# Linear attention with adaptive layer norm and an MLP: kv from sums of normalised rows, and a planned k and q stage

## The chip, the core and the metric

The kernel runs on one core of a Trainium2 chip. Five engines work side by side, each through its own instructions in order: TensorE (PE; its weight loads are PEld), VectorE (DVE), ScalarE (ACT), GpSimd (POOL) and SyncE (SP), which here issues nearly all transfers. The metric is the device time of one execution in microseconds (us), as the median of several runs.

## The reference

The input x has 2048 rows of D = 576. A vector c gives six rows of modulation by `silu(c) @ w_mod`. There are 32 heads of 18 columns; phi(t) is t + 1 above zero and exp(t) below, plus 1e-6.

```python
mod = silu(c) @ w_mod                       # sa, ca, ga, sb, cb, gb
h = layernorm(x) * (1 + ca) + sa
q, k, v = split(h @ wqkv)                   # 32 heads of 18
kv = einsum("bhsd,bhse->bhde", phi(k), v)   # per head 18 x 18
z = einsum("bhsd->bhd", phi(k))
o = einsum(phi(q), kv) / (einsum(phi(q), z) + 1e-6)
x = x + ga * (o @ wo)
h = layernorm(x) * (1 + cb) + sb
x = x + gb * (silu(h @ w1) @ w2)            # w1 is 576 x 4608
```

Everything is fp32 at the interface. The large products are made from operands that are split into a rounded high part and a remainder ("hi" and "lo"), and three products of the parts.

## The kernel before

Rows are worked in 16 tiles of 128 (`NT`), and four tiles make a block of 512 (`NB` = 4). The 576 columns are four chunks of 128 and one of 64 (`KC` = 4). A projection of a tile is 14 passes over pairs of such parts, each on two halves of the output columns: 28 matmuls (`x_passes`, L298).

The program has four stretches.

1. **Start** (`start_of_work` on, L538). The first rows of modulation are summed for the columns `cols["a"]`, tiles 0 to 3 are normalised, and k of tiles 0 and 1 is projected while weights arrive. `load_w` (L391) loads all of `wqkv` here: k, v and q, 1.33 MB each.
2. **k, v, q** (the loop at L870). For each tile t: `k_proj` (L698), phi(k) and its split into `pk` (`k_split`, L452); `v_proj` (L703), and v's split into `vx`, six small operations on ScalarE and VectorE out of PSUM; then `kv_mm` (L723) for the tile before, ten matmuls of 256 columns that gather v^T phi(k) over all 16 tiles in three PSUM tiles, `kvp`; and one `q_proj` (L718), whose phi goes to `acc[t]`. In between, the next block's rows are loaded (`load_block`), normalised, turned by 32x32 transposes and a way through DRAM (`turn_block`, L353: four stores, eight fetches), modulated and split into `hT` (`turn`, L747). The other rows of modulation are made by the way: `mod_piece` (L654) sums five scaled pieces of `w_mod` on VectorE and stores them to DRAM, `mod_sum` (L670) gathers them back in runs of nine elements and adds them up, giving `vec`. `find_first` (L838) reads all of two groups' MLP weights to find the scale factors.
3. **End of attention** (L926 to L1006): the last `kv_mm`, the mask and the row z from the PSUM sums, `kvm`, and M = kvm x (wo x ga) in five steps (L991 to L1000), with q of tiles 8 to 10 in between.
4. From L1011 on, the output of attention, its second layer norm and the MLP. The MLP's second part is emitted by a list scheduler, `Schedule` (L1832): each operation is added with an engine, a time that the planner counts for it, names that it reads and writes, and a lag for transfers. `emit` runs a model of the five engines and issues, on each, the ready operation with the earliest due time; TensorE keeps the order given.

In stretches 1 to 3 the order on TensorE is the order of the program text (`manual_schedule`). The orders on the other engines are lists of numbers written out by hand, `FIRST` (L99) for stretches 1 and 2 and `ORDERS` (L67) for what follows. An engine works strictly in that order: an instruction that waits holds those behind it.

Of the kernel before, what the change touches and what calls it, by code (L numbers as in the profile page):

```python
# [24 lines left out]
def kernel(ctx: ExitStack, tc, A_x, A_wqkv, A_wo, B_x, B_w1, B_w2, c, w_mod, out):  # L25
# [33 lines left out]
    def behind(instructions):  # L59

        with ExitStack() as order:
# [7 lines left out]
            0 2-3 5 4 1 6-12 16-18 14 13 15 19-21 23-25 32-33 26 34 22 27 44-46 28-30 40 53 35 54-55 31 36 63 47  # L69
            64-65 37-39 72 48-51 73 41 56 74 52 82 57-58 66 59-61 83-84 94 62 67 95 42 68-70 75 96 106 71 76 43 107  # L70
            77 86 80 108 81 85 88 87 78 92 79 89-91 115-116 97 93 117 126 98-102 127 103-105 109 128 145 110 146
            111-112 114 113 118 147 164-165 119-121 123-124 122 132 131 129 134 125 139 133 138 130 142 150-151 141
            161 166 162 135-136 152-153 137 163 167 154-155 173-175 156 168 158 160 172 143-144 148-149 176 157 159
            177 140 182 169-171 178-179 185 181 180 183-184 187-191 186 195 192 194 196 193 197-201 205 204 203 202
            206-207 210 209 208 211 225 229 212 221-223 233 230 234 236 235 227-228 237 214-215 238-240 216 213
            217-220 245 224 241 244 231-232 249 246 226 248 247 250 252 251 257 261 242-243 254-255 258 256 253
            259-260 262-263 265 264 268 266-267 269 273 270-272 278 274-277 281 280 282-285 279
        """,
        "Activation": """
            0-5 7 6 8-10 12 11 13-18 20 19 25-26 21 24 22-23 28-29 32 30-31 41 34 36 38 40 33 35 42 45 43 37 39 44 27  # L80
            46 48 50 52 47 53 49 51 54-57 60 58-59 69-70 62 64 66 71-73 68 61 63 65 67 74-77 81 83 82 84 79 78 85-87
            89 95 80 90 88 100-104 91-92 97 99 93-94 105 96 98 106-108 110 112-113 109 111 114 119-120 116 118 115
            117 121 123 122 124-125 127 129-131 128 126 132-134 144 146 136-138 135 139-143 145 147 150-153 156
            148-149 157-160 166 171 161-164 167 154-155 169-170 168 165 174 173 175 172 176-179 181 180 182-183 185
            187-189 186 190-192 184 194 193
        """,
        "Pool": """
            4 0-3 5-10 17 11 14 12-13 18 15-16 21 19-20 25 22-23 28 31 26-27 34 29 24 30 38 32-33 41 35-36 44 39-40
            68 56 37 42-43 60 45-46 63 47-48 51 57 52 58 49 53 50 55 54 61-62 59 64-66 78 67 69 73-75 70 76 71 77 72
            84 83 86 88 85 87 91-92 82 79 89-90 94 93 97 95-96 98-99 101 80 103 100 104 102 106 81 105 107-111  # L90
        """,
        "SP": """
            0-1 4-6 2-3 8-9 7 10-12 15 13-14 16-18 25 22 20 19 21 27-28 24 26 23 29-32 34 33 36-37 35 40 49 39 41-42
            38 43-47 50-51 53 52 48
# [6 lines left out]
            0 2 1 4-5 3 6-21 24-25 22-23 26 28 27 29-30 43-44 31-32 46 33-34 47 35-37 40 38 45 48-49 39 41-42 51 50  # L101
            53 52 55 54 56-58 61 60 62 88 63 89-90 64-65 68-69 71-72 70 73-75 77-78 76 79-80 91 66-67 81-87 93 59 92
            94-96 152 97 99-101 103-104 106-107 98 110-112 102 105 109 113-114 108 127-128 130-131 129 132-133 116
            134 136-137 135 138-139 115 117 140-141 119 142 120 143 121 144-146 118 122-123 153-154 124-125 155 126
            147-151 156-159 161 160 162-164 193-194 196-197 195 198-200 165 202-203 201 204-205 167 171 206-207 168
            208-212 172-174 166 175 169-170 176-184 190-191 185 192 213-215 186 219 216-217 223 187 218 220 224 221
            234 222 238 188-189 231-233 235-237 240-248 225 249-253 230 254-257 239 227 226 258-259 228 260 229
            261-263
        """,
        "Activation": """  # L110
            0-4 6-7 5 8-10 13 11-12 14-18 21 19-20 22-25 27 29 31 30 32 26 28 34 33 41-43 37 39 36 48 38 40 50 52 44
            46 56 45 57 47 49 58 51 53 35 59 54-55 60-62 65-67 70 73 63 68 64 77 71 78 69 79 75 72 80 76 81 74 82-83
            85 91 86 92 87 84 88-90 93-99 104 101 100 102 107 103 105 111 108 112 116 106 117 109 126-127 113-115 110
            118-125 128-130 133 138 134 140 131 139 144 132 141 149 135 145 136 150 137 142-143 146-148 151-170
        """,
        "Pool": """
            0-1 3-4 2 6-7 5 8-12 15-17 13-14 18-20
        """,
        "SP": """
            0-31 33 32 62 34-38 40-41 39 42-45 48-49 47 46 63-65 50-53 66 54 56-57 55 70-73 58-61 67-68 78-79 84-88  # L120
            90-91 89 92-95 80-82 69 74-77 83 96 99 98 100-102 97 106 103-105
# [87 lines left out]
    warm = pa.tile([P, 1], F32, name="warm")  # L209
    crowp = pa.tile([P, P], F32, name="crow")  # L210
    crow = crowp[: KC + 1]
    fixed = const.tile([P, 8], F32, name="fixed")
    BOUNDS, ALPHA, SINV, GINV = fixed[:, 0:2], fixed[:, 2:3], fixed[:, 3:4], fixed[:, 4:5]
# [18 lines left out]
    wkvs = [t[:, i * 2 * D : (i + 1) * 2 * D] for t, n in ((w7, 3), (w5, 2), *((t, 2) for t in wg2)) for i in range(n)]  # L232
    wq = wqp.tile([P, 2 * KC + 1, D], F32R, name="wq")


    class LayerNorm:


        def __init__(self, pool):
            self.mv = pool.tile([P, 4, 2], F32, name="mv")  # L240
            self.ve = pool.tile([P, 4], F32, name="ve")
            self.rstd = pool.tile([P, 4], F32, name="rstd")
            self.nm = pool.tile([P, 4], F32, name="nm")
            self.pool = pool
# [70 lines left out]
    def wkv(b):  # L315

        return wkvs[b]

    def wqp_(b):
        return wq[:, b, :]  # L320
# [4 lines left out]
    kvp = [psA.tile([P, 2, 256], F32, name=f"kvp{i}") for i in range(3)]  # L325

    def psT():
        t = psA.tile([P, 512], F32, name="psT")
        return t
# [5 lines left out]
    def rows4():  # L335
        t = pa.tile([P, 4, DX], F32, name="xt")
        return t

    def load_x(i):
        xt = x0[:, i]  # L340
        nc.sync.dma_start(xt[:, :D], x[i * P : (i + 1) * P, :])
        return xt

    def load_block(tb):
        xx = rows4()
        for a in range(4):
            src = x[tb * 512 + a * P : tb * 512 + (a + 1) * P, :].rearrange("(t j) d -> j t d", t=4)
            nc.sync.dma_start(xx[32 * a : 32 * a + 32, :, :D], src)  # L350
        return xx

    def turn_block(tb, xx):  # L353

        sq = accb[NB - 1].rearrange("p a d -> p (a d)").rearrange("p (f q) -> p f q", q=P)
        for t in range(4):
            V.transpose(sq[:, :, 32 * t : 32 * t + 32], xx[:, t, :D].rearrange("p (f i) -> p f i", i=32))
        room = dram.tile([32, D // 32, 4, P], F32, name=f"turned{tb}")
        for a in range(4):
            nc.sync.dma_start(room[:, :, a, :], sq[32 * a : 32 * a + 32])  # L360
# [45 lines left out]
    for j in (1, 2):  # L406
        load_w(j, START)
# [1738 lines left out]
```

## Time and profile before

| | |
|---|---|
| median of 3 runs | 1129.71 us (1128.67 to 1131.22) |
| the profiled execution | 1127.2 us |
| its span, first to last instruction | 1125.5 us |
| TensorE's granted clock, mean | 0.994 |
| busy: PE, DVE, ACT, POOL | 1083.3, 899.7, 692.8, 662.5 us |
| stretches 1 to 3 end (first transpose of the attention output) | 238.1 us |

The page of the profile lists the busy time of each engine, the granted TensorE clock, the chain of work that ended last, and the costliest groups of instructions as "line engine op out<-in xcount | busy, mean ns | idle before, and what ended it". The table by stretches gives busy time by engine for any part of the span. A wait is put down to the one thing that came last. Lines are those of the kernel before.

### The profile page before, as it was taken

The page shows a single profiled execution, that of the slowest core. Times are in us where ns is not written, and L with a number is a line of the kernel's source. Part 1 is how long each engine was busy: PE and PEld are TensorE (multiplying, and loading weights), DVE is VectorE, ACT ScalarE, POOL GpSimd, SP SyncE. Part 2 cuts the span into 40 slices and gives each one's busy share as a digit, 9 for nine tenths or more (in the row PEclk, how much of TensorE's full clock was granted, in tenths as well). Part 3 has the DMA queues.
Part 4 walks back from the last instruction along what each step waited for, and adds up shares of the span by engine and source line. Part 5 has one row for each costly group of instructions (what it writes and reads, how often), then busy time and mean ns, then how long its engine had stood idle before and what let it go on. Part 6 is the DMA issues. An engine that isn't in the chain of part 4 may idle for free.

```text
span 1125.5 us, 19357 instructions
## 1 busy us (share of the span) xinstructions
PE 1083.3 (96%) x7137; PEld 778.4 (69%) x7137; DVE 899.7 (80%) x1478; ACT 692.8 (62%) x1336; POOL 662.5 (59%) x759
## 2 busy tenths in 40 slices
PE   8999799999999997999999999999999999999998
PEld 6899798899888554566666666666666666666665
DVE  7757574678698889989898888897897897898857
ACT  4643452244755668777677677686686686676654
POOL 3300000065462468968979858878778778777563
PEclk9999899999999999999999999999999999999999
DMA  9376958223344565858757757747757657725522
GB/s 293 81 198 156 129 139 105 43 67 112 122 102 139 200 232 174 281 129 262 205 183 224 219 166 242 223 147 240 215 156 241 219 149 240 222 82 176 172 86 106
DMA packets 120079, 193.53 MB, mean 172 GB/s; under 512 B 43372, under 2 KB 78064, under 8 KB 119984
## 3 DMA queue, kind: packets, MB, share of 16 engines
q1 hardware_dynamic: 119812, 191.99, 58.9%
q8 instruction: 56, 0.92, 0.4%
q14 instruction: 39, 0.32, 0.1%
q10 hardware_dynamic: 172, 0.30, 0.1%
HBM read 176.77 MB, written 15.48 MB: 171 GB/s over the span
## 4 chain that ended last, share of the span: by engine, by line
PE 75%; DMA 8%; DVE 6%; POOL 4%; ACT 4%; issue 1%; SPq 1%; POOLq 0%; ACTq 0%; DVEq 0%
PE up L1595 29%; PE down L1679 28%; PE big L302 7%; PE psK L302 4%; DMA z<-in_B_w_dram 2%; DMA acc<-in_A_wqkv_dram 2%; PE small L1103 1%; DMA xt<-in_A_x_dram 1%; PE big L1114 1%; DMA turned<-acc 1%; PE psK L997 1%; PE big L1028 1%; PE small L287 1%; DVE st L249 1%; PE kvp L729 1%
## 5 line engine op out<-in xcount | busy, mean ns | idle before, releaser
L1595 PE MATMUL up<-hT,w 128*128 128x512 f16 x1264 | 316.7, 380 | 8.3 <-DMA hT<-hd 3.3
L1595 PEld LDWEIGHTS <-w 128*128 128x128 f16 x1492 | 146.1, 98 | 142.5 <-issue 9.7
L1688 DVE SCALAR_TENSOR_TENSOR acc<-acc,set,down 128x576 f32<-128x576 f32 x128 | 103.5, 810 | 33.8 <-PE down L1679 32.9
L302 PE MATMUL psK<-w,hT 128*128 128x256 f32 (+1 forms) x638 | 106.8, 305 | 14.2 <-DVE vx L177 13.1
L1613 ACT ACTIVATE f<-f,set 128x512 f32<-128x512 f32 x102 | 73.3, 719 | 61.5 <-DVE f L1619 51.5
L1633 POOL TENSOR_TENSOR s<-f,f 128x256 f32<-128x256 f32 x66 | 54.8, 830 | 92.0 <-ACT f L1614 89.7
L302 PEld LDWEIGHTS psK<-w,hT 128*128 128x128 f32 x638 | 95.4, 197 | 15.4 <-issue 14.0
L1679 PE MATMUL down<-w,hb 128*128 128x288 f16 x600 | 88.9, 286 | 2.5 <-DVE U L1690 1.7
L1679 PE MATMUL down<-w,hc 128*128 128x288 f16 x600 | 88.9, 286 | 0.2 <-DVE acc L1692 0.2
L1679 PE MATMUL down<-w,hT 128*128 128x288 f16 x480 | 82.8, 286 | 0.4 <-DVE acc L1692 0.4
L1617 DVE TENSOR_TENSOR f<-up,p 128x512 f32<-128x512 f32 x102 | 69.6, 682 | 13.7 <-PE up L1595 8.3
L1679 PEld LDWEIGHTS <-hb 128*128 128x128 f16 x600 | 58.7, 98 | 24.6 <-issue 2.8
L1614 ACT ACTIVATE f<-f,set 128x512 f32<-128x512 f32 x102 | 73.6, 722 | 3.3
L1679 PEld LDWEIGHTS <-hc 128*128 128x128 f16 x600 | 58.7, 98 | 21.9 <-issue 0.5
L255 POOL TENSOR_TENSOR rstd<-ve,neghalf 128x4 f32<-128x4 f32 (+3 forms) x10 | 9.9, 993 | 103.4 <-DVE ve L254 102.3
L1657 POOL TENSOR_TENSOR hc<-s,hc 128x512 f16<-128x512 f32 x50 | 63.1, 1262 | 5.6 <-ACT hc L1653 5.6
L1619 DVE TENSOR_TENSOR f<-up,f 128x512 f32<-128x512 f32 x68 | 46.8, 688 | 24.5 <-PE up L1595 23.8
L1679 PEld LDWEIGHTS <-hT 128*128 128x128 f16 x480 | 47.0, 98 | 26.6 <-issue 0.8
L1637 POOL TENSOR_TENSOR f<-f,s 128x256 f32<-128x256 f32 x66 | 53.0, 803 | 17.1 <-DVE hb L1657 9.4
L1630 POOL TENSOR_TENSOR s<-f 128x256 f32<-128x256 f32 x66 | 56.3, 853 | 7.2 <-ACT f L1610 4.8
L1635 POOL TENSOR_TENSOR s<-s,f 128x256 f32<-128x256 f32 x66 | 56.6, 857 | 3.5
L1679 PE MATMUL down<-w,hd 128*128 128x288 f16 x396 | 55.1, 288 | 0.0
(381 smaller groups left out, 2698.2 us busy)
## 6 DMA issues: line engine op xcount, KB each, us to landing
hT<-hd SPq DMA_DIRECT2D x101, 640.0 KB, 4.7
hT<-hd SPq DMA_DIRECT2D x65, 512.0 KB, 4.0
hT<-in_B_w_dram SPq DMA_DIRECT2D x14, 576.0 KB, 6.7
hT<-in_B_w_dram SPq DMA_DIRECT2D x28, 256.0 KB, 6.3
raw<-in_B_w_dram SPq DMA_DIRECT2D x9, 576.0 KB, 6.8
v<-in_B_w_dram SPq DMA_DIRECT2D x9, 576.0 KB, 4.9
xt<-in_A_x_dram SPq DMA_DIRECT2D x16, 288.0 KB, 5.5
raw<-in_w_mod_dram SPq DMA_DIRECT2D x8, 576.0 KB, 7.8
```

The lines of the kernel that those rows point to most:

```text
L302: T.matmul(ps, xpart(a), wpart(b), start=n == 0, stop=n == len(XW) - 1)
L1595: T.matmul(ps, left, right, start=first and m == 0, stop=m == len(seq) - 1, skip_group_check=True)
L1613: A.activation(f, f, AF.Silu, scale=factor(self.g, "inv"))
L1614: aside(A.activation(f, f, AF.Identity, scale=factor(self.g, "delta")))
L1617: V.tensor_add(f, self.bank[bank[1]], self.p1)
L1630: G.tensor_sub(self.s3, half(i, 0, 0), half(i, 0, 1))
L1633: G.tensor_add(self.s[:, 0:1], half(i, 0, 1), half(i, 1, 1))
L1635: G.tensor_sub(self.s[:, 1:2], self.s[:, 0:1], half(i, 0, 0))
L1637: G.tensor_sub(half(i, 1, 0), half(i, 1, 0), self.s[:, 1:2])
L1657: eng.tensor_sub(t[:, :, 1, :], src, t[:, :, 0, :])
L1679: T.matmul(ps[:, p, :HALF], left[:, u, p * P : (p + 1) * P], right[:, v], start=n in (1, 5, 7, 6) and j == 0, stop=j == len(passes) - 1, s ...
L1688: V.scalar_tensor_tensor(dst, dst, factor(self.g, "ratio"), ps[:, :, :HALF], op0=ALU.mult, op1=ALU.add)
```

## The change

Since v = h Wv, and h is a normalised row times (1 + ca) plus sa, the sum of v^T phi(k) over rows can be made without v. The changed kernel sums, over all rows, the products of normalised rows (before modulation) and phi(k): a 576 x 576 matrix in five tiles `sums_of`, in SBUF. It applies (1 + ca), the term of sa times z, and Wv once, at the end. In detail:

- `v_proj`, `vx` and `kv_mm` go. `split_rows` splits the normalised rows of a block into hi and lo (`xs`), one ScalarE copy and two subtractions per tile, the wide one on VectorE for two tiles and on POOL for two.
- After the k tiles of a block, `sum_steps` makes five chunks of 24 (or 16) matmuls of 288 columns over its four tiles, in two PSUM tiles `psG` by turns, and adds each to `sums_of`.
- `zsum` collects phi(k) by POOL adds; `z_steps` sums it over partitions by a matmul with ones, and corrects `sums_of` by z times sa.
- `kv_steps` multiplies with Wv in fp32: 25 matmuls of 126 columns. Wv is loaded late (`load_late`), so only the weights of k and q are loaded at the start.
- `mod_steps` scales the pieces of `w_mod` on ScalarE and adds them on POOL, where `mod_piece` did both on VectorE.
- Stretches 2 and 3 are emitted by `Schedule`, which moves up in the text unchanged. TensorE's order is: q0, q1, k2, k3, q2, sums of block 0, q3, k4 to k7, q4, sums of block 1, k8 to k11, q5 to q7, sums of block 2, k12 to k15, q8, sums 0 and 1 of block 3, z, sums 2 to 4, q9, kv, q10, M.
- A tile of x or PSUM is used again under names: x of the next block may load when `split_rows` and the transposes have read the last; `xs` is written again when the sums have read it; k and q tiles use two PSUM tiles, K0 and K1, by turns.
- Blocks 1 to 3 keep their rows in another order (`rows_of`), also where x is loaded again and the result is stored; the MLP's `store` is two transfers in place of one.
- The lists `FIRST` and `ORDERS` are shorter by what the planner has taken over.

In the order that this gives, the gather of the first modulation piece stands on SyncE after the store of turned block 2 and ahead of its eight fetches, and its reduction (into `crow`) on VectorE between the two modulates and the five splits of block 2. The gather of the second piece stands behind block 3's fetches, six scan loads and the store of the parts; its reduction stands on VectorE between the first phi operation (PSUM to `a`) of k12 and its second, ahead of those of k13.

The diff, cut to its core:

```diff
-    for j in (1, 2):
-        load_w(j, START)
+    load_w(1, START)
...
+    def project(t, wpart):
+        ps, k = k_bank()
...
+            pe(0.264 * n, product, [x for x in names if x.split(".")[1][0] == str(c)], [k])
+    def phi_steps(ps, k, out, names):
+        do("ACT", 0.65, lambda: A.activation(halves(e_), ps[:, :, :HALF], AF.Exp), [k], ["e"])
+        do("DVE", 0.75, lambda: V.tensor_scalar(halves(out), ps[:, :, :HALF], 0.0, EPS, op0=ALU.max, op1=ALU.add), [k], names)
+        do("DVE", 0.79, lambda: phi_out(e_, out), ["e"], names)
+    def k_steps(t):
...
+        do("ACT", 0.68, lambda: A.copy(pk[i][:, 0], a), [an], [f"pkh{i}"])
+        by_pool = i < 2 or t == 2
+        eng, us = (G, 1.6) if by_pool else (V, 0.75)
...
+        do("POOL", 1.6, lambda: G.tensor_add(zsum, zsum, a), [an], ["zsum"])
+    def split_rows():
+        C = KC * P
+        for t in range(4):
+            do("ACT", 0.68, lambda t=t: A.copy(xs[t][:, :D], xt[:, t, :D]), [f"xt{t}"], [f"xhi{t}"])
+            eng, us = (V, 0.7) if t < 2 else (G, 1.35)
...
+    def block_steps(b):
+        for t in range(4):
+            do("SP", 0.1, lambda t=t: nc.sync.dma_start(xt[:, t, :D], rows_of(x, 4 * b + t)), [], [f"xt{t}"], 6.5)
...
+        do("SP", 0.4, store, SQ, [f"turned{b}"], 4.7)
+        do("SP", 0.4, fetch_main, [f"turned{b}"], XT, 4.5)
+        do("SP", 0.4, fetch_tail, [f"turned{b}"], [XTAIL], 5.5)
+    def sum_steps(b, c):
+        ps, g = g_bank()
...
+                    T.matmul(ps[:, h, :HALF], l, pk[t][:, u, h * HALF : (h + 1) * HALF],
+                             start=t == 0 and m == 0, stop=t == 3 and m == len(left) - 1)
...
+    def mod_steps(piece):
...
+                do("ACT", 1.25, lambda raw=raw, kp=kp, scale=scale: A.activation(raw[:kp], raw[:kp], AF.Identity, scale=scale), [], raws2[i])
+                do("POOL", 2.7, lambda raw=raw, dst=dst, kp=kp: G.tensor_add(dst, dst, raw[:kp]), raws2[i], ["tmod"])
+        do("SP", 0.1, lambda: nc.sync.dma_start(parts, tmod2[:, :, 0:D]), ["tmod"], [f"parts{piece}"], 5.5)
+        i = next(of_raw) % 2
+        r = raw2[i].rearrange("q a d -> q (a d)").rearrange("q (p j) -> q p j", j=NC9)
+        do("SP", 0.1, lambda: nc.sync.dma_start(r, parts.rearrange("p a d -> p (a d)").rearrange("p (q j) -> q p j", j=NC9)),
+           [f"parts{piece}"], raws2[i], 8.0)
+        s9 = s9s[piece - 1]
+        do("DVE", 2.27, lambda: V.tensor_reduce(s9, r.rearrange("q p j -> q j p"), axis=AX.X, op=ALU.add), raws2[i], [f"s9{piece}"])
...
+    def kv_steps():
+        ps, g = g_bank()
+        def product(j):
+            n = HG if j < NHC - 1 else TAIL
+            o = ps[:n, 0, j * HG : (j + 1) * HG] if j < NHC - 1 else ps[:n, 1, :n]
+            for c in START:
+                T.matmul(o, wvs[c][:, j * HG : j * HG + n], sums_of[c][:, j * HG : j * HG + n], start=c == 0, stop=c == KC)
...
         def store(self, b, i, k):
-            t0 = (4 * b + 2 * i) * P
-            dst = of[t0 : t0 + 2 * P, k * HALF : (k + 1) * HALF]
-            nc.sync.dma_start(dst.rearrange("(i p) d -> p i d", p=P), self.c(b, i, k))
+            for u in range(2):
+                nc.sync.dma_start(rows_of(of, 4 * b + 2 * i + u, slice(k * HALF, (k + 1) * HALF)), self.c(b, i, k)[:, u])
```

848 lines of the change are left out of this document (460 added, 388 removed).

## The prediction

> **What bounds the kernel now.** I read the page first, then the chain that ended last, then the table by stretches of the first 238 us (the part that changes), TensorE's waits there, and SyncE's queue in order of time. Page and stretches (columns: us, then busy us and instruction count of PE, PEld, DVE, ACT, POOL, then clock, DMA share, GB/s):
>
> ```profile
> span 1125.5 us, 19357 instructions
> PE 1083.3 (96%) x7137; PEld 778.4 (69%) x7137; DVE 899.7 (80%) x1478; ACT 692.8 (62%) x1336; POOL 662.5 (59%) x759
> 75.00:100.00 25.00, 22.09 (x166) 21.68 (x166) 20.73 (x39) 8.81 (x19) 1.37 (x1) 1.00 0.47 145
> 100.00:120.00 20.00, 15.28 (x118) 15.08 (x116) 8.28 (x14) 7.18 (x16) 0.00 (x0) 1.00 0.88 177
> 120.00:136.80 16.80, 14.11 (x95) 13.90 (x95) 11.80 (x29) 7.24 (x15) 1.29 (x1) 0.90 1.02 110
> 136.80:186.00 49.20, 49.20 (x361) 49.07 (x362) 31.72 (x48) 20.06 (x42) 2.34 (x5) 0.97 0.79 128
> 186.00:220.30 34.30, 29.64 (x209) 28.82 (x208) 18.59 (x43) 8.58 (x22) 0.60 (x1) 0.95 0.33 78
> sum 204.70, PE 187.81 PEld 182.91 DVE 128.98 ACT 81.20 POOL 22.59; mean PE 23.48 PEld 22.86 DVE 16.12 ACT 10.15 POOL 2.82
> 120.00:125.00 5.00, 5.00 (x26) 5.00 (x27) 4.84 (x16) 3.60 (x7) 0.00 (x0) 0.66 1.77 60
> PE psK L302 <- DVE vx L177: 13.1, 4, 4.7
> 136.80 9.20 PE psK L302 x56
> 146.00 1.19 PE kvp L729 x10
> 147.18 7.49 PE psK L302 x56
> 225.37 2.21 PE psK L997 x8
> 231.31 6.80 PE psK L997 x28
> 238.11 0.55 PE big L1028 x5
> ```
>
> TensorE bounds it. The sum row (33.4 to 238.1 us) has it busy for 187.81 of 204.70 us; its 16.9 idle us lie in a few holes, 13.1 of them behind VectorE's v rows. A hole is paid twice: after the 4.7 us one the granted clock is 0.66 for 5 us (1.7 us lost), and the first 56 matmuls after another take 9.20 us where 7.49 is usual. From 238.11 on, the attention output and the MLP follow; the change leaves their work alone, so I move 238.11 and keep the rest.
>
> **The change, part by part.**
>
> TensorE's work. A projection of one 128-row tile is 28 matmuls, half of the 7.49 row: 3.74 us. The 16 v projections go; the 16 tiles' sums cost 28 matmuls of 288 columns each: the same, so nothing. The 16 kv groups of 10 go: 16 x 1.19 = 19.0 us. Added: 25 fp32 matmuls of 126 columns for kv. The chain's L997 rows show fp32 as two instructions per matmul, at 2.21/8 = 0.276 us with 288 columns; five 128-column transposes take 0.55, 0.11 each. So 50 instructions cost 5.5 to 13.8 us; I take 6.0, as 0.276 x 126/288 = 0.12 lies by the lower row. The z row stays two such matmuls. Net -13 us.
>
> In the new order TensorE has 14 k and 11 q projections (93 us), 16 sum tiles (60), M (2.21 + 6.80 = 9.0), kv 6.0, z 1.1, ten transposes 1.1: 170 us. It starts with transposes of tiles 2 and 3, which wait for this row:
>
> ```profile
> 28.11 2.29 ACT L264 ACTIVATE xt<-xt,nm,rstd 128x64 f32<-128x64 f32 x4
> 29.29 0.28 PE L302 MATMUL psT<-w,hT 128*128 128x256 f32 x1
> ```
>
> so at 30.4 (before, the first v tile, the PE row, began at 29.3), and without holes M would end near 200.5. The rest is holes: TensorE takes its instructions in the listed order, and so do the others, so a wait at the head of VectorE's or SyncE's queue holds whatever stands behind it. These rows price the chains that make them (groups by form, the table of DMA issues, the chain, SyncE's queue):
>
> ```profile
> L177 DVE TENSOR_TENSOR hT<-acc,hT 128x512 fp32r<-128x512 f32 x12 | 8.2, 688 | 3.9 <-ACT hT L278 3.8
> L437 DVE TENSOR_SCALAR a<-psK 128x576 f32<-128x576 f32 x15 | 11.3, 755 | 15.2 <-ACT e L432 15.0
> L665 DVE SCALAR_TENSOR_TENSOR tmod<-raw,sc,tmod 128x1152 f32<-128x1152 f32 x6 | 8.5, 1412 | 0.0
> L675 DVE TENSOR_REDUCE s<-raw 128x9 f32<-128x1152 f32 x2 | 4.5, 2266 | 0.0
> L272 ACT ACTIVATE acc<-acc,col_a 128x512 f32<-128x512 f32 x12 | 9.5, 812 | 1.1 <-DMA acc<-turned 1.1
> L422 POOL TENSOR_TENSOR wq<-acc,wq 128x576 fp32r<-128x576 f32 x4 | 6.4, 1618 | 6.7 <-ACT wq L417 6.7
> L255 POOL TENSOR_TENSOR rstd<-ve,neghalf 128x4 f32<-128x4 f32 x3 | 3.7, 1220 | 81.0 <-DVE ve L254 81.0
> xt<-in_A_x_dram SPq DMA_DIRECT2D x12, 288.0 KB, 6.1
> parts<-tmod SPq DMA_DIRECT2D x2, 576.0 KB, 7.4
> raw<-parts SPq DMA_DIRECT2D x2, 576.0 KB, 12.8
> 60.98 0.32 SPq L365
> 67.99 1.52 ACT acc L272 x2
> 92.19 3.56 SPq L360 DMA_DIRECT2D turned<-acc  x4
> 99.69 1.76 SPq L365 DMA_DIRECT2D acc<-turned  x4
> 116.08 0.39 SPq L673 DMA_DIRECT2D raw<-parts  x1
> 116.52 10.85 SPq L373 DMA_DIRECT2D raw<-in_w_mod_dram  x2
> 171.65 0.61 SPq L779 DMA_DIRECT2D z<-in_B_w_dram  x1
> 174.67 0.38 SPq L673 DMA_DIRECT2D raw<-parts  x1
> 175.09 10.98 SPq L742 DMA_DIRECT2D raw<-in_A_wo_dram  x3
> ```
>
> Read: first store of a turned block to first fetch is 7.5 us (92.19 to 99.69), fetch to modulated rows 7.0 (60.98 to 67.99). The gather of the modulation parts lands after 12.8 us, and both times SyncE's next issues stand for about 11 us behind it.
>
> Block 1. Its x tiles can load only when the splits have read block 0's; the last leaves at about 42.6 and lands at 48.7; statistics, power, normalising and transposes follow to 55.3; the store waits 0.9 us behind a modulation load that waits for POOL's first add; 7.5 and 7.0 more give 70.7. VectorE's two modulates and the five splits at 0.69 then pace TensorE: the first tile ends at 77.6, 3.7 us late; with 1.3 at the second q tile, whose PSUM bank is emptied on VectorE behind the first splits of x, 5.0 us of holes.
>
> Block 2. Its loads wait for the splits of block 1, which wait for block 0's sums (66.5) and stand on VectorE behind the modulates: 72.8, landed 79. VectorE's queue has k7's phi (88.8) ahead of the second normalising, POOL's power stands behind one add of the parts (3.0, from 1618 x 1152/576) and four 576-wide operations: transposes end at 94.5, the fetch is due at 102. But the gather is ahead of it: POOL's last add at 92.9, the parts landed at 100.3. SyncE is held to 111.7, so modulation starts at 116, and the parts' reduction (2.27) stands between VectorE's modulates and its splits: 116 + 1.4 + 2.3 + 5 x 0.69 = 123.2. TensorE ran out of work at 107.4; k8 ends at 125 with the low clock: 13.9 us of holes.
>
> Block 3 is nearly hidden: q5 to q7 and 15 us of sums cover its chain; 0.3 us.
>
> The second gather. k11 ends at 136; POOL's power behind two adds and four operations: 142; transposes 145.3; fetch issued from 152.8 (eight issues, 3.5 us); six scan loads at 0.6 each; parts store 159.9, landed 167.3, gather landed 180.1. Its reduction stands on VectorE behind k12's first phi half, ahead of all that empties k13's PSUM bank: 180.1 + 2.3 + two 0.76 = 184, and the last k tile ends at 189.5 instead of 177.4 (1.7 for the clock in it): 12.1 us.
>
> ScalarE has two scan squares (some 1.6 us each, 812 x 1024/512) ahead of k12's exponential, which wait for loads that land near 164; the exponential ends at 169, and its bank is wanted at 170: nothing, and 1 us for each us that the loads are later. Behind the gather the k13 exponential waits as VectorE does, for the same 184.
>
> Tail. q8, the last sums, z, q9, kv, q10 and M are 42 us of TensorE; a bank of sums costs about 1.5 more. Sum: 200.5 + 5.0 + 13.9 + 0.3 + 12.1 + 1.5 = **233.3**, 4.8 us before 238.1. Reckoned from the other side (238.1, less 13 of work, the old holes of 16.9, and 4.9 of lost clock from the stretches' clock column; plus the new 32.8 and 1.1 of later start) M ends at 237.2; the 3.9 between are time that neither side names. I take the first, whose every term has a place, and leave the other to the range.
>
> Edits at nothing. VectorE loses the v rows and the modulation sums and gains the splits of x, the sums' evictions and their correction by z: by the rows above about 134 us in place of 128.98, in 200; as a load it bounds nothing, only its order does. The modulation sums leave VectorE (8 to 13 us: L665's six and four more, not shown) for ScalarE (ten of 1.35) and POOL (eight of 3.0): POOL's 22.59 us become about 83, still under half of the stage, and where it sets an end, ahead of the powers, I counted it. The v weights' six loads move from the first 28 us to about 185, under q8 and the sums; uncovered, about 6 us, as the x row of the same 288 KB. Nine scan loads in place of fourteen spare SyncE 3 us where it waits anyway. The rows of x come back to the accumulators permuted, with the same bytes; 0. The MLP's split stores add issues of 0.4 us to a queue that waits; 0.
>
> The profiled execution took 1127.2, 2.5 under the median 1129.71. Its 1127.2 - 4.8 is 1122.4; as a median, **1125**.
>
> **The rivals.**
>
> The gathers stay hidden. The planner in the diff counts 8.0 us for a gather. If fetches pass it and it lands in 8: modulation at 109.5, without the reduction in the way, k8 ends near 115.5 (9.5 saved), the second hole shrinks by about 6: M at 218, 1110. For it: only two gathers stand in the trace. Against it: both held SyncE 11 us.
>
> Slower: POOL stretches. Every block's power stands behind POOL work that before did not exist: 9.4 us in block 2, 12.6 in block 3, each on the path. If its operations take 1.5 times their 1618 ns with VectorE busy beside them, 11 us are added: M at 244, 1136. It decides from 4.8/22, a stretch of 1.22. Rows on it:
>
> ```profile
> 450.00:700.00 250.00, 247.19 (x1561) 152.52 (x1560) 218.25 (x332) 178.42 (x355) 203.11 (x237) 1.00 0.71 211
> L1379 POOL TENSOR_TENSOR ht<-ht,sl 128x512 f32<-128x512 f32 x2 | 3.4, 1719 | 0.0
> ```
>
> Against it: both engines work through most of those 250 us (421 together). For it: 512 wide there took 1719 ns, where 1618 x 512/576 would be 1438: 1.2 times, just on the edge. I keep 1618, since it was taken in this stage beside a busy VectorE. The Trainium skill speaks for this rival (SBUF — State Buffer, "SBUF: two separate sides"): GpSimd and a VectorE operation with two SBUF inputs take a shared port pair exclusively, for whole instructions, and the other blocks. The new VectorE and POOL work is mostly of that kind; by the rule the sum would be this rival's 1136, by the row 1125; the trace agrees in part (1.2 times, no full exclusion).
>
> The change doesn't do what it says: kv's 19 us return because VectorE's order, not TensorE, paces every block; that is my two large holes grown by 5 us, 1130.
>
> **How the numbers follow.** The forecast (holes as above, 1118 to 1130): 0.42; hidden gathers (1102 to 1117): 0.29; stretched POOL (1131 to 1145): 0.22; order paces all (about 1130): 0.07. About 0.2%, 2.3 us, is what a measurement here can tell from no change. Of the forecast's chance, 0.35 lies under 1127.4: faster 0.64, the same 0.13 (0.07 and edges), slower 0.23. The range 1104 to 1138 reaches into both rivals, and holds kv's upper bound (+7.8). The forecast's own range is 1118 to 1130.
>
> **What would show it.** No PE rows for v or L729; 16 sum tiles at 3.74 us; kv near 6 us; a hole of about 10 us ahead of the k tiles of block 2 with the gather just landed, and one of about 10 ahead of the last k tile, put down to VectorE; first output transposes near 233. It is wrong if the fetches pass the gather, if POOL's 576-wide adds take over 2 us, or if the holes stand elsewhere.

## The result and the profile after

| | before | after |
|---|---|---|
| median | 1129.19 us, 4 runs | 1158.72 us, 4 runs (1158.3 to 1158.93) |
| profiled execution; its span | 1127.2; 1125.5 us | 1158.3; 1156.6 us |
| first output transposes start | 238.1 us | 251.2 us |
| VectorE's last instruction ends | 1122.8 us | 1137.6 us |
| from there to the end of the span | 2.7 us | 19.0 us |

The changed kernel is slower: the ratio is 1.026, with a 95% interval from 1.0242 to 1.0278. The forecast was 1125 and its range ended at 1138. In the profiled executions 31.1 us came on, in two places: 13.1 us ahead of the first output transposes, and 16.3 us behind VectorE's last instruction. Between them, in the attention output and the MLP, there are 1.8 us (the sum agrees within rounding).

**The end.** This is the table of DMA use of the kernel after, from 1112 us on, in 40 slices of 1.2 us. A digit is the mean busy share of 16 DMA engines in tenths.

```profile
DMA  0022222100000022222222222222222222200000
GB/s 0 9 64 97 89 78 97 63 1 0 0 0 0 0 23 27 75 98 104 104 102 106 100 104 104 102 106 100 104 104 100 108 97 97 97 22 0 7 0 0
```

The same stretch of the kernel before:

```profile
DMA  0381746619000000000000000000000000000000
GB/s 0 134 351 19 307 163 253 257 75 386 33 0 0 0 0 0 0 0 0 0 0 0 0 0 0 0 0 0 0 0 0 0 0 0 0 0 0 0 0 0
```

Before, 2.38 MB leave here and after 2.98 MB, since the same stores come later; most are transfers of 288 KB. Before, they go in bursts of up to 386 GB/s and are done 2.7 us after VectorE. After, the flow stands at 97 to 108 GB/s with a quarter of the engines busy ("2"; 0.26 as a mean from 1138 to 1154 us), and the stores pile up until the span ends at 1156.6.

**The first stretches.** From 28 us to the first output transposes, the table of windows (length, then busy us and instructions of PE, PEld, DVE, ACT, POOL, then granted clock, DMA share, GB/s) of the kernel before:

```profile
28.00:238.11 210.11, 192.51 (x1371) 187.38 (x1371) 132.73 (x254) 86.00 (x178) 22.60 (x22) 0.98 0.60 120
```

and of the kernel after:

```profile
28.00:251.18 223.18, 186.34 (x1251) 179.66 (x1251) 150.76 (x247) 87.54 (x139) 82.74 (x56) 0.91 0.56 119
```

TensorE's idle time went from 17.6 to 36.8 us, 19.2 more. Its busy time fell by 6.2 us only, with the clock down from 0.98 to 0.91. 19.2 less 6.2 is the 13.1 lost, within rounding. VectorE has 18 us more to do. What TensorE waited for, after (total us, times, longest):

```profile
PE psK L846 <- ACT hT L896: 13.1, 2, 10.0
PE psK L846 <- ACT e L852: 7.5, 1, 7.5
PE psG L951 <- DVE w L864: 5.8, 3, 4.2
PE psG L951 <- ACT w L861: 2.9, 2, 2.4
PE psG L951 <- DVE sum L961: 2.5, 1, 2.5
```

The chain that ended last names the causes of these in order of time (start, length):

```profile
42.02 11.63 DMA xt<-in_A_x_dram
...
115.81 8.31 SPq L928
...
132.27 2.17 DVE crow L1002
...
145.87 11.30 DMA xt<-in_A_x_dram
...
189.01 7.87 SPq L648
...
233.62 5.04 PE psG L1079 x50
...
251.18 0.55 PE big L1236 x5
```

A block's loads of x land 11.6 and 11.3 us after the issue, where the row of before had 6.1. Block 2's fetch stands 8.3 us behind the first gather, and the reduction into `crow` stands behind the modulates: the forecast's first large hole, as it was described. The second hold, 7.9 us, is on the scan loads.

### The profile page after: what moved, and what is told of

It is laid out like the page before. It is cut to its first block, busy times and chain, and to the rows that moved or that the text cites. A ratio compares the mean times of both kernels' runs of the same rounds, so it can differ in the third digit from the quotient of the medians.

```text
span 1156.6 us, 19138 instructions
## 1 busy us (share of the span) xinstructions
PE 1080.4 (93%) x7027; PEld 773.2 (67%) x7027; DVE 915.8 (79%) x1467; ACT 695.6 (60%) x1300; POOL 722.1 (62%) x789
## 4 chain that ended last, share of the span: by engine, by line
PE 74%; DVE 9%; DMA 6%; ACT 4%; SPq 2%; POOL 2%; issue 1%; DVEq 0%; ACTq 0%; POOLq 0%
PE up L1803 29%; PE down L1887 28%; PE big L295 6%; PE psK L846 2%; DMA xt<-in_A_x_dram 2%; DMA acc<-turned 2%; PE psG L951 1%; PE small L1311 1%; DMA turned<-acc 1%; PE big L1322 1%; SPq L928 1%; DVE hT L167 1%; PE psK L1116 1%; DVE a L406 1%; SPq L648 1%
## 5 line engine op out<-in xcount | busy, mean ns | idle before, releaser
L1803 PEld LDWEIGHTS <-w 128*128 128x128 f16 x1492 | 146.3, 98 | 143.5 <-issue 11.3
L846 PE MATMUL psK<-w,hT 128*128 128x288 f32 x308 | 51.9, 322 | 21.5 <-ACT hT L896 13.1
L1845 POOL TENSOR_TENSOR f<-f,s 128x256 f32<-128x256 f32 x66 | 53.4, 810 | 17.2 <-DVE hb L1865 10.1
L846 PEld LDWEIGHTS psK<-w,hT 128*128 128x128 f32 x308 | 48.1, 212 | 22.7 <-ACT hT L896 13.5
L951 PE MATMUL psG<-w,xs 128*128 128x288 f32 x336 | 52.3, 313 | 2.6 <-DVE sum L961 2.5
```

What stands on the lines that cost most here:

```text
L846: T.matmul(o, part(a), w(b), start=c == 0 and m == 0, stop=c == KC and m == 1)
L951: T.matmul(ps[:, h, :HALF], l, pk[t][:, u, h * HALF : (h + 1) * HALF], start=t == 0 and m == 0, stop=t == 3 and m == len(left) - 1)
L1803: T.matmul(ps, left, right, start=first and m == 0, stop=m == len(seq) - 1, skip_group_check=True)
```

## The experiments

"Transposes" is the start of the first output transposes, "tail" the time from VectorE's last instruction to the end of the span; both are from each run's profile. The ratio is to runs of the kernel before on the same chip.

| run | transposes | tail | median us | ratio to before (95%) |
|---|---|---|---|---|
| before | 238.1 | 2.7 | 1129.19 | |
| after | 251.2 | 19.0 | 1158.72 | 1.0242 to 1.0278 |
| e1_stores | 252.6 | 10.5 | 1150.08 | 1.0142 to 1.0229 |
| e7_before_rows | 237.1 | 18.3 | 1143.66 | 1.0116 to 1.0159 |
| e12_before_eight | 237.4 | 7.7 | 1132.55 | 1.0028 to 1.0057 |
| e2_loads | 238.1 | 18.6 | 1144.30 | 1.0111 to 1.0182 |
| e3_all | 240.1 | 10.1 | 1144.74 | 1.0112 to 1.0185 |
| e11_one_load_four | 245.1 | 19.0 | 1151.87 | 1.0197 to 1.0229 |
| e5_plain_rows | 247.5 | 3.4 | 1137.45 | 1.0062 to 1.0108 |
| e9_one_load | 233.1 | 3.4 | 1126.49 | 0.9981 to 1.0009 |
| e8_no_gather | 231.3 | 3.4 | 1121.20 | 0.9887 to 0.9949 |
| e4_all_hold | 230.7 | 10.1 | 1134.42 | 1.0043 to 1.0091 |
| e6_plain_rows_hold | 239.9 | 3.3 | 1129.21 | 0.9998 to 1.0026 |
| e10_one_load_hold | 231.0 | 3.4 | 1121.49 | 0.9926 to 0.9954 |
| e13_no_zsum | 246.5 | 19.0 | 1152.61 | 1.0208 to 1.0239 |
| e15_zsum_writes | 245.0 | 19.1 | 1151.22 | 1.0201 to 1.0231 |
| e14_no_pool_sums | 244.1 | 18.5 | 1149.04 | 1.0176 to 1.0213 |

### The tail: the pattern of the stores

`rows_of` takes a tile of blocks 1 to 3 as four runs of 32 rows, so the transfer's access pattern has an outer dimension of 4.

e1_stores writes each store as four transfers of 32 rows:

```diff
-            nc.sync.dma_start(rows_of(of, a, c), acc[a][:, c])
+            for p, rows in quarters(of, a, c):          # 32 rows each
+                nc.sync.dma_start(rows, acc[a][p, c])
```

> The changed kernel, with each output store of the MLP written as four transfers of 32 rows in place of one whose outer dimension is 4. Theory A (a transfer with an outer dimension of 4 is carried by 4 of the 16 DMA engines, and the stores pile up behind each other at the end): the last transfer ends about 3 us after VectorE's last instruction in place of 19, so about 1142.5 us (1139 to 1146), and the first output transposes stay at 251. Rival B (the number of store issues and their turn in SyncE's queue sets the tail): with four times as many issues the time is 1158 or more.

The tail nearly halved, to 10.5 us, and the time fell by 8.6 us, to 1150.08, between the two theories. Neither holds alone: 36 issues stand in SyncE's queue where the kernel after had 9, and the last leaves 8 us behind VectorE's end (the queue's timeline: start, length from the first issue to the end of the last):

```profile
1128.70 18.01 SPq L1937 DMA_DIRECT2D out_dram<-acc  x36
```

One issue takes 0.42 us at the median, 15 us for the 36. So pattern and number of issues could not be told apart here, and the next two runs put the pattern into the kernel before, where nothing ahead of the stores changes:

```diff
-            nc.sync.dma_start(of[a * P : (a + 1) * P, c], acc[a][:, c])
+            nc.sync.dma_start(rows_of(of, a, c), acc[a][:, c])
```

> The kernel before, with its output stores alone written through the changed kernel's row pattern (outer dimension 4) and the paired stores in two; nothing ahead of them is touched, and the rows of the output land in other places than the reference's. Theory A: the tail after VectorE's last instruction grows from 2.7 to about 19 us, 1142 to 1146 us. If the tail came from the changed kernel's later order and not from the pattern: 1127 to 1131.

> As e7_before_rows, with an outer dimension of 8 in place of 4 in the stores of the kernel before (rows of the output in other places than the reference's). If the number of DMA engines follows the outer dimension, a store takes about half as long, VectorE's pace is nearly met and the tail falls from 18.3 us to 2.7 to 6: 1127 to 1132 us. If a broken run of rows costs the same however it is broken: 1141 to 1146.

With an outer dimension of 4 the kernel before takes 1143.7 us and has a tail of 18.3: the end of the changed kernel, in the kernel before. With 8 the tail is 7.7 us, longer than the 2.7 to 6 expected, and the time 0.55 us above its range. The table of DMA use from 1112 us on, of e7_before_rows:

```profile
DMA  0002222222222222222222220000000000000000
GB/s 0 0 0 25 42 83 104 100 104 104 102 106 100 104 104 102 104 102 102 106 102 98 97 87 6 0 7 0 0 0 0 0 0 0 0 0 0 0 0 0
```

and of e12_before_eight:

```profile
DMA  0003455455555520000000000000000000000000
GB/s 0 0 0 44 111 186 188 185 184 204 205 207 176 198 77 14 0 0 7 0 0 0 0 0 0 0 0 0 0 0 0 0 0 0 0 0 0 0 0 0
```

A quarter of the engines' time and about 103 GB/s at 4, a half and about 200 at 8 (mean shares of 0.26 from 1120 to 1139 us and 0.52 from 1118 to 1128): the share of the DMA engines at work follows the outer dimension. As 4.2 and 8.3 of 16 engines, this is an estimate from the shares, since the trace does not name the engines. The Trainium skill states this as a rule (DMA: Bandwidth & Descriptors, "Why a DMA increments its semaphore by 16 and not by 1"): a transfer uses the largest number of engines up to 16 that divides the slowest dimension (other than one of size 1) of both access patterns. These traces agree, with 2 and 5 tenths.

### The first stretches: loads and order

e2_loads loads a block as the kernel before does. Its four transfers of 32 partitions are also one operation for the list scheduler, where there were four, and so the order changes too:

```diff
-        for t in range(4):
-            do("SP", 0.1, lambda t=t: nc.sync.dma_start(xt[:, t, :D], rows_of(x, 4 * b + t)), [], [f"xt{t}"], 6.5)
+        def load():
+            for a in range(4):
+                src = x[b * 512 + a * P : b * 512 + (a + 1) * P, :].rearrange("(t j) d -> j t d", t=4)
+                nc.sync.dma_start(xt[32 * a : 32 * a + 32, :, :D], src)
+
+        do("SP", 0.4, load, [], [f"xt{t}" for t in range(4)], 6.5)
```

> The changed kernel, with a block of x loaded by four transfers of 32 partitions (as the kernel before does) in place of four with an outer dimension of 4; the stores stay as they are. Theory A: a block's load lands in about 6 us in place of 11.5, the blocks' chains are some 5 us shorter, and the first output transposes come 5 to 13 us earlier (238 to 246 in place of 251.2); the kernel takes 1146 to 1154 us, with the 19 us tail of stores still there. Rival C (the gathers and the order hold the first stretches, the loads are beside them): the first output transposes stay within 1.5 us of 251 and the time within 1157 to 1160.

> Both edits together, and the reload of x into the accumulators in four transfers of 32 rows too. Theory A: the two gains add, 16 + 5 to 13 us, so 1130 to 1138 us, and what is left above the forecast of 1125 lies in the stretches ahead of the first output transposes. If the forecast's other terms were right as well, the transposes stand near 233 and the time near 1125. Rivals B and C: 1155 or more.

In e2_loads the transposes came 13.1 us earlier, and the time is just under its range. In e3_all the gains did not add, and the time is 1144.7 where 1130 to 1138 was expected: the transposes are at 240.1 and the tail at 10.1, but from the transposes to VectorE's end it takes 893.9 us where e2_loads takes 886.3. Two edits touch that stretch. The stores in quarters leave it at 885.7 in e1_stores, so most of the 7.6 us is put down to the reloads of x in quarters; no run has these alone, and in e4_all_hold, which has both too, the stretch takes 891.1.

Two edits were mixed in e2_loads. e5_plain_rows gives the loads and stores whole rows and keeps the order; e11_one_load_four changes the order alone; e9_one_load does both:

```diff
     def rows_of(y, t, c=slice(0, D)):
-        b = t // 4
-        if b == 0:
-            return y[t * P : (t + 1) * P, c]
-        return y[b * 512 : (b + 1) * 512, c].rearrange("(a t j) d -> t a j d", a=4, t=4)[t % 4]
+        return y[t * P : (t + 1) * P, c]
```

> The changed kernel with one function altered: rows_of gives 128 rows in a run for every tile, so block loads, reloads and output stores each move a run of 128 rows with one transfer of outer dimension 128; nothing else is touched, and the number of transfers is the same. Theory A (the outer dimension of 4 costs both the loads' 5 us per block and the tail of stores): the first output transposes at 236 to 240 as with the loads alone, the tail after VectorE's last instruction about 3 us, and 1124 to 1129 us in all, which is the forecast's time. If the number of transfers mattered too, the tail would stay above 8 us and the time above 1131.

> The changed kernel with its own row pattern kept for loads, reloads and stores (outer dimension 4), and only the four loads of a block given to the scheduler as one operation. Theory O: most of the 13 us of e2_loads is here, transposes at 238 to 243, and with the tail of 19 us 1144 to 1150. If the loads' 5 us per block were the cause: transposes at 249 to 253, 1156 to 1161.

> As e5_plain_rows, with a block's four loads of x given to the list scheduler as one operation (as in e2_loads), so that only the planner's order changes. Theory O (the order decides: with one operation the first gather is issued ahead of block 2's store and no fetch stands behind it): first output transposes at 236 to 240 in place of 247.5, 1125 to 1130 us. If the 13 us of e2_loads came from its way of loading by quarters of partitions: transposes at 245 to 249, 1135 to 1139.

Whole rows alone bring the transposes 3.7 us forward and the tail to 3.4 us; the expectations of 236 to 240 and of 1124 to 1129 us were misses. Order alone brings them 6.1 us forward, less than expected. Both together bring 18.1 us, more than expected: the parts do not add, because the order decides what stands behind a gather, and the loads decide how much the order can gain. In e9_one_load the gather is issued at 80.75, and block 2's fetch leaves at 110.54 with nothing ahead of it (SyncE's queue):

```profile
80.75 0.38 SPq L999 DMA_DIRECT2D raw<-parts  x1
...
110.54 1.76 SPq L928 DMA_DIRECT2D acc<-turned  x4
```

In the kernel after the same two are 111.87 and 115.81, and the first fetches take 9.74 us to issue:

```profile
111.87 1.30 SPq L999 DMA_DIRECT2D raw<-parts  x1
115.81 9.74 SPq L928 DMA_DIRECT2D acc<-turned  x4
...
186.37 10.98 SPq L648 DMA_DIRECT2D acc<-in_B_w_dram  x2
```

### The gathers

e8_no_gather is e5_plain_rows, in its order, with each gather replaced by a plain load:

```diff
-        do("SP", 0.1, lambda: nc.sync.dma_start(r, parts.rearrange("p a d -> p (a d)").rearrange("p (q j) -> q p j", j=NC9)),
+        do("SP", 0.1, lambda: nc.sync.dma_start(raw2[i], parts),
            [f"parts{piece}"], raws2[i], 8.0)
```

> As e5_plain_rows, with the two gathers of the modulation's parts (16384 pieces of 36 bytes each) replaced by plain loads of the same bytes, so that the modulation vectors are wrong and only the time counts; the reductions on VectorE stay. The forecast's holes (13.9 us in block 2, 12.1 us ahead of the last k tile, both behind a gather): the transposes come 15 to 25 us earlier than in e5_plain_rows (213 to 224) and the time falls to 1100 to 1113. If the blocks' own chains of load, statistics, transposes and fetch set the pace, less than 8 us earlier.

The transposes came 16.2 us earlier, 247.5 to 231.3, at the lower end of what the forecast's two holes would give; the total, 1121.2, is above the expected range, since those 16 us started from 247.5.

The three "hold" runs tell the planner what the queue does:

```diff
-        do("SP", 0.1, lambda: nc.sync.dma_start(r, ...), [f"parts{piece}"], raws2[i], 8.0)
+        do("SP", 11.5, lambda: nc.sync.dma_start(r, ...), [f"parts{piece}"], raws2[i], 1.5)
```

> As the run before it, and the list scheduler is told that a gather of the modulation's parts keeps SyncE for 11.5 us (0.1 us before) so that it can put other transfers ahead of it. Theory D (the transfers queued behind the two gathers cost the forecast's 13.9 and 12.1 us of holes): the first output transposes come 3 to 10 us earlier than in the run before it. Rival E (the list scheduler has nothing better to put there, or the holes are of another cause): within 1.5 us of it, or later.

> As the run before it, with the list scheduler told that each gather keeps SyncE for 11.5 us. If that is worth what it was with the split stores (transposes 8 to 9 us earlier): transposes at 228 to 232 and 1115 to 1121 us, below the kernel before. If it was an accident of that order: 1124 to 1129, as the run before it.

> The run before it with the planner told that a gather keeps SyncE for 11.5 us. If the gains add as in e4_all_hold (transposes at 230.7 there) and the reloads and stores of whole rows cost what they cost in e5_plain_rows: transposes at 229 to 232, 1116 to 1121 us, some 0.8% under the kernel before. If an order is worth nothing that another change does not take back: 1125 or more.

On e3_all it gave 9.4 us at the transposes, on e5_plain_rows 7.6, on e9_one_load, whose first gather stood well already, 2.1. The gain in e6_plain_rows_hold was the expected one, but from 247.5 and not from 238, so it ended above its range, level with the kernel before. e10_one_load_hold takes 1121.49 us, just above its range and 0.994 of the kernel before (0.9926 to 0.9954): with whole rows, one load operation per block and a true price for the gather, the idea is worth 0.6%.

### POOL beside VectorE

VectorE's groups of phi and of the split of phi(k) in the kernel before (busy us, mean ns of one):

```profile
L441 DVE SCALAR_TENSOR_TENSOR a<-e,a 128x576 f32<-128x576 f32 x16 | 12.4, 772 | 0.4
L177 DVE TENSOR_TENSOR pk<-a,pk 128x576 fp32r<-128x576 f32 x16 | 12.0, 752 | 9.6 <-ACT pk L453 9.5
```

and after:

```profile
L406 DVE SCALAR_TENSOR_TENSOR a<-e,a 128x576 f32<-128x576 f32 x16 | 17.0, 1060 | 1.1 <-ACT e L852 0.7
L864 DVE TENSOR_TENSOR w<-a,w 128x576 fp32r<-128x576 f32 x7 | 8.9, 1270 | 1.1 <-ACT w L861 1.1
L909 DVE SCALAR_TENSOR_TENSOR mv<-mv 128x2 f32<-128x2 f32 x6 | 6.4, 1060 | 0.0
```

Two rows of the kernel after show it happen: an operation of 128 x 2 on VectorE, whose shortest took 148 ns, begins beside a POOL add and ends with it, 2.63 us later.

```profile
98.72 2.63 DVE L909 SCALAR_TENSOR_TENSOR mv<-mv 128x2 f32<-128x2 f32 x1
```

```profile
98.52 2.81 POOL L995 TENSOR_TENSOR tmod<-tmod,raw 64x1152 f32<-64x1152 f32 x1
```

Three runs of the kernel after, all orders kept, take POOL's adds away or replace them:

```diff
-        do("POOL", 1.6, lambda: G.tensor_add(zsum, zsum, a), [an], ["zsum"])
+        do("POOL", 1.6, lambda: None, [an], ["zsum"])                                          # e13, e14
+        do("POOL", 1.6, lambda: [G.memset(zsum, 0.0) for _ in range(3)], [an], ["zsum"])       # e15
...
-                do("POOL", 2.7, lambda raw=raw, dst=dst, kp=kp: G.tensor_add(dst, dst, raw[:kp]), raws2[i], ["tmod"])
+                do("POOL", 2.7, lambda: None, raws2[i], ["tmod"])                              # e14
```

> The changed kernel with its order on every engine kept, and POOL's adds of phi(k) into zsum left out (14 of 1551 ns; z is then wrong). Nothing but z waits for them. Theory P (POOL's adds and VectorE's operations with two SBUF inputs hold each other up, and POOL's powers stand behind the adds): the second half of phi(k) on VectorE falls from 1060 ns towards 850, the split of phi(k) on VectorE from 1270 towards 900, and the first output transposes come 4 to 10 us earlier (241 to 247). Rival (POOL's adds are hidden): transposes within 1.5 us of 251.2.

> The changed kernel with each add into zsum replaced by three POOL writes of zeros into it (about 1.6 us together, so POOL's queue is as long; they read nothing from SBUF; z is then wrong). If the stretch on VectorE comes from POOL reading SBUF beside it: VectorE's groups fall as in e13_no_zsum, and the transposes come 2 to 8 us earlier than 251.2. If the adds cost through POOL's queue ahead of the powers: VectorE's groups may fall, but the transposes stay within 1.5 us of 251.2. If any POOL work stretches VectorE: groups stay at 1060 and 1270.

> As the run before it, and POOL's adds of the modulation parts (some 2.8 to 3 us each) left out as well, so that the modulation is wrong. Theory P: the two groups on VectorE within 100 ns of the kernel before (772 and 752), no 128 x 2 operation above 1 us, VectorE's busy time ahead of the transposes at 134 to 140 us in place of 150.8, and the transposes at 232 to 243. Rival: VectorE's times stay, and the transposes move by less than 3 us or only as far as the parts' earlier store moves the gather.

The transposes came 4.7, 6.2 and 7.1 us earlier. With both kinds of adds gone (e14_no_pool_sums), VectorE's operations are back at their times of before, and its busy time is 132.9 us in the window to the transposes, slightly under the expected range, with the transposes, at 244.1, slightly late of theirs:

```profile
28.00:244.06 216.06, 184.73 (x1265) 178.74 (x1264) 132.94 (x251) 89.55 (x142) 38.58 (x34) 0.92 0.58 123
L406 DVE SCALAR_TENSOR_TENSOR a<-e,a 128x576 f32<-128x576 f32 x16 | 12.7, 794 | 1.1 <-ACT e L852 0.7
L864 DVE TENSOR_TENSOR w<-a,w 128x576 fp32r<-128x576 f32 x7 | 5.2, 742 | 1.1 <-ACT w L861 1.1
```

The parts of the modulation are stored earlier in e14_no_pool_sums, at 81.9 us instead of 101.4, but the gather still goes out 3.7 us behind block 2's store, as in the kernel after, so the earlier parts do not explain the gain.

e15_zsum_writes keeps POOL as busy (84.13 us against 82.74) with writes that read nothing, and gains no less than e13_no_zsum, which takes the same adds out. In block 1 the reason can be read directly. POOL's powers begin at 55.30 us where the kernel after has 55.52, so it is not POOL's queue ahead of the powers. Two of VectorE's operations behind them differ. In the kernel after they are

```profile
57.84 1.61 DVE L864 TENSOR_TENSOR w<-a,w 128x576 fp32r<-128x576 f32 x1 [0.38 <-ACT w L861]
59.38 2.60 DVE L909 SCALAR_TENSOR_TENSOR mv<-mv 128x2 f32<-128x2 f32 x1
```

and in e15_zsum_writes

```profile
57.62 0.76 DVE L864 TENSOR_TENSOR w<-a,w 128x576 fp32r<-128x576 f32 x1 [0.38 <-ACT w L861]
58.30 0.15 DVE L909 SCALAR_TENSOR_TENSOR mv<-mv 128x2 f32<-128x2 f32 x1
```

So VectorE is done with them 3.5 us earlier, and the store of the turned rows leaves at 62.3 instead of 65.2 us. That part of the gain comes from adds that read SBUF beside VectorE. For the later blocks the run does not separate this from another effect: an add waits for phi(k) (27.2 us of POOL's idle time in the kernel after), and a write of zeros does not. The groups did not fall one by one as expected: in e13_no_zsum the split of phi(k) even rose to 1703 ns (its longest, 3.07 us, ran beside an add of the modulation parts), and what fell most was the operation of 128 x 2 (1060 to 147 ns) and with it the sum, 150.8 to 145.8 us.

## Why the prediction was wrong, by its steps

**"The rows of x come back to the accumulators permuted, with the same bytes; 0. The MLP's split stores add issues of 0.4 us to a queue that waits; 0."** This step failed: the stores cost 16.3 us where it has 0, which alone would have made the change slower. The bytes are the same, but the pattern leaves a transfer about a quarter of the DMA engines. At the end nothing covers it, shown in both directions by e5_plain_rows (tail 3.4) and e7_before_rows (18.3). The split as such cost next to nothing: e5_plain_rows keeps it. The forecast named no work that hides the last stores, and its "from 238.11 on the change leaves their work alone" was true of the engines only.

**The sum, 233.3.** This failed too, and without the tail it would still have turned the sign: the transposes began at 251.2. Of the 17.9 us between, 15.4 were lost before TensorE ran out of work ahead of block 2, 0.1 in block 2, and 4.1 from the end of k8 to the end of the last k tile; the rest came 1.7 us faster than forecast.

**The x loads at the 6.1 us row.** The row belonged to transfers of another pattern. The changed loads take 11.3 to 11.6 us; with whole rows (e5_plain_rows) the loads of block 1 land after 3.8 us at the median. Alone they are worth 3.7 us at the transposes, and more with another order.

**TensorE's work, -13 us.** Right. A sum tile is 3.73 us (64 matmuls in 8.52 in the chain), kv took 5.04 us (forecast 6.0, with 5.5 as the lower bound). The 179.5 us of work that 192.5 - 13 leaves were seen where the holes are small: 179.5 in e9_one_load and 181.4 in e10_one_load_hold. In the kernel after it is 186.3, some 7 us more, at a clock of 0.91 (0.93 and 0.95 in those two). That the clock is the reason is likely and was not separated; the forecast had counted a low clock only inside its large holes.

**Block 1.** Here the time was lost first, before any gather. The first k tile of block 1 ended at 86.4 us instead of 77.6, and TensorE ran out of work ahead of block 2 at 122.8 instead of 107.4. So 15.4 of the 17.9 us were there before the first large hole. In them are the late loads, VectorE's stretch, the clock, and a wait that no step had: the sums wait for the split of phi(k), 8.7 us in all (`w` in the waits), 7.9 of them here. The longest, 4.2 us, comes about because VectorE's queue has the next block's normalising and transposes ahead of the split. Taken away alone, POOL's adds (e14_no_pool_sums) let TensorE run out at 115.6 us, 7.2 earlier, and the changed row pattern (e5_plain_rows) at 120.5, 2.3 earlier.

**"VectorE ... by the rows above about 134 us."** Failed as a duration: the forecast added 5 us to the kernel before (counted from 33.4 us on), and from 28 us on 18.0 came on, 132.7 to 150.8. As a count of operations it was nearly right, since without POOL's adds it is 132.9.

**Block 2 and the first gather, 13.9 us.** Right in place, mechanism and size: from 122.8 us to the end of k8 at 140.5 (forecast 125), less the tile's 3.7 us of work, are 14.0 us. TensorE was idle for 10.0 behind the modulated rows and 1.0 more behind the split, and the rest went at a low granted clock, 0.73 from 125 to 150 us.

**The second gather, 12.1 us.** Right in place and in what carries it, smaller. TensorE was idle for 7.5 us, and the last k tile then took 6.0 us instead of 3.7, so 9.8 in all. The idle time is put down to ScalarE's exponential of k13, but that one waited last for VectorE, whose first phi operation of k13 stands behind the reduction, as forecast (VectorE's timeline, with the idle time before each):

```profile
198.78 2.20 DVE L1002 TENSOR_REDUCE crow<-raw 128x9 f32<-128x1152 f32 x1 [9.78 <-DMA raw<-parts]
200.90 0.75 DVE L406 SCALAR_TENSOR_TENSOR a<-e,a 128x576 f32<-128x576 f32 x1
201.56 0.75 DVE L853 TENSOR_SCALAR a<-psK 128x576 f32<-128x576 f32 x1
```

ScalarE had a wait of its own, shorter by 0.97 us only. A scan square waits for a scan load that SyncE holds behind the gather, and the exponential of k13, the last row here, is queued behind the square (ScalarE's timeline):

```profile
200.28 1.06 ACT L649 ACTIVATE acc<-acc 128x1024 f32<-128x1024 f32 x1 [10.20 <-DMA acc<-in_B_w_dram]
201.25 0.19 ACT L649 ACTIVATION_READ_ACCUMULATOR acc<-acc 128x1 f32 x1
202.40 0.65 ACT L852 ACTIVATE e<-psK 128x576 f32<-128x576 f32 x1 [0.97 <-DVE a L853]
```

The forecast had weighed such a wait for k12, as "nothing, and 1 us for each us that the loads are later". Moving the reduction alone would therefore have gained little here; no run tried it. Without the gathers 16.2 us go, where the forecast had 26.

**The tail of 43.8 us from the last k tile to the transposes.** Right: 209.1 to 251.2, 42.1.

**The rivals.** "The gathers stay hidden" is out: they cost 16.2 us in this order. For the first gather it does come about in another order: in e9_one_load and e10_one_load_hold no fetch stands behind it. The second still holds SyncE there: in e10_one_load_hold the two scan loads behind it take 11.44 us to issue. "POOL stretches" was turned down because POOL's own operations would hold their pace. They do: the adds of 576 columns took 1551 ns, below the 1618 assumed. It is VectorE that is stretched, by 18 us of work (150.8 against 132.9 without the adds), and taking the adds away is worth up to 7.1 us at the transposes. The rule weighed there (the Trainium skill, SBUF — State Buffer, "SBUF: two separate sides") says that either engine may be the one that waits. The trace agrees, with 2.63 us for an operation of 148 ns. The rule's side of that weighing was the better one for the first stretches, though it gave 1136 by the wrong engine. "Order paces all" is partly true, as VectorE's queue ahead of the sums shows.

That e9_one_load ends at 1126.5 with its transposes at 233.1, next to the forecast's 1125 and 233.3, is luck and no proof of the forecast: its holes are others (14.1 us behind the modulated rows, 7.2 behind the split of phi(k), none of 12 at the last k tile).

What stays open: how the 15.4 us in front of block 2 divide between the loads, VectorE's stretch, the order and the clock. POOL's adds and the row pattern were taken away alone, for 7.2 and 2.3 us; the clock was not. Loads and order interact (3.7 and 6.1 us alone, 18.1 together, at the transposes), so no division would be unique.

## What to carry to other kernels

Price a moved transfer by its access pattern, not by its bytes: look at the outer dimension on both sides, and name the work that covers it, for the last stores above all. Tell a list scheduler how long a queue is held, not only when the data lands, and read its order for what stands behind such a transfer. Work given to POOL had a second price on VectorE here, so look at the two engines' rows side by side where both read SBUF.

## What the runs showed of the hardware

- Stores with an outer dimension of 4, 8 and 128 ran at about 103, about 200 and up to 386 GB/s, with 2, 5 and up to 9 tenths of the DMA engines busy. Loads of x of the same size took 11.3 to 11.6 us with an outer dimension of 4 and 3.8 at the median with 128.
- Splitting each store in four had a price in issues: 36 issues of 0.42 us at the median stood in SyncE's queue for 18 us, and the tail was 10.5 us, against 3.4 for whole rows.
- A VectorE operation of 128 x 2, whose shortest took 148 ns, took 2.63 us beside a POOL add and ended with it. With POOL's adds into `zsum` replaced by writes of zeros of about the same length, all six of its kind took 147 ns in the mean, and the output transposes began 6.2 us earlier.
